# A fused linear-attention and feed-forward kernel: new ranks for its start, filling counted with two lengths, a last slice in two halves

## The chip, the cores and the metric

The kernel runs on one core of a Trainium2 chip. The metric is the device time of one execution in microseconds, here the median of 3 runs. A profiled execution stands beside it: its own time, its span (first to last instruction) and a trace of every instruction on the engines: TensorE (PE; its weight loads PEld), VectorE (DVE), ScalarE (ACT), GpSimd (POOL) and SyncE (SP), which issues most of the transfers.

## The reference

Two stages follow one another. The first is a linear attention with a decay `w` per head and channel and a bonus `u` for the current token, over 4 sequences of 768 tokens with 8 heads of 48 channels:

```python
for t in range(S):
    cur = np.einsum('bhd,bhe->bhde', u[None] * kt, vt)
    y[:, :, t] = np.einsum('bhd,bhde->bhe', rt, state + cur)
    state = w[None, :, :, None] * state + np.einsum('bhd,bhe->bhde', kt, vt)
```

The second takes its output as 3072 tokens of 384 features:

```python
h = x @ w_in                       # 384 -> 2048
g = h * np.clip(h + 3.0, 0.0, 6.0) / 6.0
return g @ w_out                   # 2048 -> 384
```

## The kernel before, in words

**Attention.** The sequence is cut into 12 chunks of 64 tokens, and each chunk into two halves (two of the four sequences each), which gives 24 steps `attention(i)`. A step scales `r` and `k` by powers of `w` (`RP`, `ks`: two products of 112x512), on the first eight steps forms their product for the bonus (`X`), scales `k` for the state (`KH`), and then has PE do two groups of small products: `first` (scores, half of the state's update, the bonus, the old state's share) and `second` (scores times `v`, the rest of the update). Between the two, DVE puts the bonus on the diagonal (L365) and copies the masked scores (L416). After `second`, DVE scales the state (`St`, L420), ACT and DVE write the step's output as a high and a low part (`x`, L429 and L430), and on the odd steps six small transfers (L439) move rows of `x` into place.

**Feed-forward.** A product in full precision is made of three products of parts: high by high, low by high, high by low. The hidden width is cut into 16 slices `f` of 128, the tokens into 6 groups `g` of 512. A unit `n` is one slice of one group. `ffn1` computes `h` with nine products (L169), ACT the rectified `t` (L457), DVE the gate (L459), ACT the high part of `g` (L461), DVE the low part (L462, recorded at the helper's L230), and `ffn2` adds nine products into three banks of PSUM (L176; bank 0 is `oa`, banks 1 and 2 are the halves of `o`). A unit of 512 tokens is in two such groups of nine products of 128x512. The first six units have 256 tokens. The weights come as 64-bit numbers; `weights(f)` loads one slice of 768 KB into `raw` and makes its high and low parts in seven operations, spread over DVE, ACT and POOL.

**What sets the order.** `Schedule` takes all of this as about 1200 operations, each with the engines that may do it and a cost on each (`add`). `order()` plays the program through with these costs, WAIT and LAND (a transfer ends LAND after its own length), and always takes on an engine the ready operation of the highest priority. The priorities of the first 561 operations are the numbers in RANKS, which reach to about the middle of the program; later ones go by the longest way to the end. The result is one fixed order for each engine. Which engine does an operation comes out of it too. SP and the engines work through their lists strictly in order.

**Filling.** Where PE has a gap of the planned order before WARM, the program puts in products that nobody reads (`warm`, L569: 128x512 in bf16 into bank `oa`), as many as fit when each lasts 0.216 us:

```python
n = int((start - free - 0.25) / 0.216)
if n > 0 and free < WARM:
```

They stand in PE's list like all else, so they are done even when the gap turns out shorter.

**The end.** The last unit is slice 15 of group 5. Its `ffn2` is done in two parts, banks 1 and 2 first and then bank 0; ACT moves bank 2 into `z` and bank 0 into `cv` (L495), DVE moves bank 1 into the other `cv` (L496), and SP sends all three (L497). After that every engine takes a branch (L601) round a fallback for unusual `w`, then SP waits for all its transfers and the engines meet at the end (L729).

Of the kernel before, what the change touches and what calls it, by code (L numbers as in the profile page):

```python
# [19 lines left out]
B, H, S, D = 4, 8, 768, 48  # L20
# [24 lines left out]
LAND = 1.8  # L45
# [134 lines left out]
def fast_path(tc, mp, pp, sb, w_hi, w_lo, b3, wm, badi, hps, o0, o12, krT, vkrt, vpt, wp, wu, wcat, out):  # L180
    nc = tc.nc
    S = Schedule()
    dma, act, dve, pool = nc.sync.dma_start, nc.scalar, nc.vector, nc.gpsimd
    eng = {"dve": dve, "pool": pool, "act": act}

    def two(name, shape, dt=F32):
        return [sb(f"{name}{q}", shape, dt, mp) for q in range(2)]
# [549 lines left out]
```

## Time and profile before

| | |
|---|---|
| median of 3 runs | 511.19 us (510.42 to 512.87) |
| the profiled execution | 511.17 us, span 509.5 us, granted TensorE clock 0.995 |
| PE busy | 494.8 us (97%), 5157 products |
| DVE busy | 300.6 us (59%) |
| ACT busy | 186.9 us (37%) |
| POOL busy | 73.2 us (14%) |
| moved by DMA | 44.38 MB |

How to read what is quoted further on. A row of the timeline is: start in us, length in us, engine, line, operation, output<-input, shapes, count, and in square brackets the idle time of the engine just before it and what ended that. A row of the chain of waits is: start, length, what the chain was doing; "issue" is time in which an engine waited for nothing that the profile shows. A row of a table by stage gives for each engine its busy us and in brackets its number of instructions that touch the stage, then the granted clock, the share of the DMA engines and GB/s. In the table of waits a row names who waited, for whom, and then us in total, how often, and the longest. In the view of one line a row has the count, then min/median/max in ns, then the first and the last start in us.

### The profile page before, as it was taken

Reading aid. Unit: us, or ns where it says so; the run is one execution under the profiler, and the core shown is the slowest. Engines: PE = TensorE matmul, PEld = TensorE weight load, DVE = VectorE, ACT = ScalarE, POOL = GpSimd, SP = SyncE. Lnnn points to the kernel's source line nnn. Section 1 sums busy time; section 2 is a strip of 40 time slices with the busy share of each in tenths; the row PEclk is TensorE's granted clock in tenths of the full one; section 3 lists DMA queues with packets and bytes.
Section 4 is the critical chain, followed back from the end, with each engine's and each line's share of the span. In section 5 each row is a group of like instructions: output and inputs, shape, how many; then the busy total and the mean of one; then the engine's idle time right before and its main releaser. Section 6 shows DMA issues by size and latency. Waiting matters only on the chain.

```text
span 509.5 us, 11797 instructions
## 1 busy us (share of the span) xinstructions
PE 494.8 (97%) x5157; PEld 393.9 (77%) x5157; DVE 300.6 (59%) x468; ACT 186.9 (37%) x295; POOL 73.2 (14%) x67
## 2 busy tenths in 40 slices
PE   9799989999999999999999999999999999999993
PEld 4566877888887888888778888778888778888882
DVE  6689999999965673534685334675333662433331
ACT  1154355556643333333233333323432333333331
POOL 1233521200001410100320001241001410000000
PEclk9999999999999999999999999999999999999997
DMA  8967573453103430200350101343100200100001
GB/s 225 263 212 218 163 225 124 161 171 124 63 0 115 132 100 1 99 0 27 119 177 8 62 1 37 103 128 100 64 0 1 99 14 15 62 1 0 1 0 68
DMA packets 14171, 44.38 MB, mean 87 GB/s; under 512 B 2561, under 2 KB 2946, under 8 KB 14114
## 3 DMA queue, kind: packets, MB, share of 16 engines
q1 hardware_dynamic: 14050, 43.50, 27.5%
q8 instruction: 42, 0.69, 0.6%
q14 instruction: 15, 0.12, 0.1%
q10 hardware_dynamic: 64, 0.07, 0.1%
HBM read 36.68 MB, written 4.72 MB: 81 GB/s over the span
## 4 chain that ended last, share of the span: by engine, by line
PE 95%; DVE 3%; issue 1%; ACT 1%; ACTq 0%
PE h L169 39%; PE o L176 25%; PE oa L176 13%; PE PP L376 10%; PE oa L569 5%; PE U L376 1%; PE o L376 1%; DVE t L459 0%; DVE z L230 0%; DVE KH L230 0%; DVE X L365 0%; DVE X L416 0%; ACT t L457 0%; PE U L325 0%; DVE z L265 0%
## 5 line engine op out<-in xcount | busy, mean ns | idle before, releaser
L169 PE MATMUL h<-x,w_hi 128*128 128x512 f32 (+1 forms) x594 | 166.8, 389 | 0.2 <-DVE t L459 0.2
L459 DVE SCALAR_TENSOR_TENSOR t<-t,h 128x512 f32<-128x512 f32 (+1 forms) x99 | 66.3, 670 | 133.7 <-ACT t L457 133.5
L176 PE MATMUL o<-g,w_hi 128*128 128x512 f32 (+1 forms) x396 | 136.2, 386 | 0.2 <-ACT g L461 0.2
L457 ACT ACTIVATE t<-h,b 128x512 f32<-128x512 f32 (+1 forms) x99 | 66.9, 676 | 187.4 <-PE h L169 187.3
L169 PEld LDWEIGHTS h<-x,w_hi 128*128 128x128 f32 x594 | 108.6, 188 | 23.4 <-DVE t L459 0.4
L230 DVE TENSOR_TENSOR g<-t,g 128x512 fp32r<-128x512 f32 (+1 forms) x99 | 69.3, 700 | 36.2 <-ACT g L461 35.7
L176 PEld LDWEIGHTS o<-g,w_hi 128*128 128x128 f32 x396 | 73.8, 188 | 16.3 <-ACT g L461 0.6
L461 ACT CAST g<-t 128x512 fp32r<-128x512 f32 (+1 forms) x99 | 60.2, 608 | 65.8 <-DVE t L459 65.7
L169 PE MATMUL h<-x,w_lo 128*128 128x512 f32 (+1 forms) x297 | 82.1, 385 | 0.0
L176 PE MATMUL oa<-g,w_hi 128*128 128x512 f32 (+1 forms) x198 | 78.3, 397 | 0.2 <-DVE g L230 0.2
L176 PE MATMUL o<-g,w_lo 128*128 128x512 f32 (+1 forms) x198 | 75.8, 383 | 0.0
L169 PEld LDWEIGHTS h<-x,w_lo 128*128 128x128 f32 x297 | 54.9, 188 | 11.6
L176 PEld LDWEIGHTS oa<-g,w_hi 128*128 128x128 f32 x198 | 37.1, 188 | 9.1 <-DVE g L230 0.7
L176 PEld LDWEIGHTS o<-g,w_lo 128*128 128x128 f32 x198 | 37.2, 188 | 7.6
L230 POOL TENSOR_TENSOR ks<-kr,IW 112x512 f32<-112x512 f32 x16 | 21.9, 1374 | 145.0 <-PE PP L376 104.9
L176 PE MATMUL oa<-g,w_lo 128*128 128x512 f32 (+1 forms) x99 | 38.0, 384 | 0.0
L376 PE MATMUL U<-vkr,KH 64*48 64x48 f32 x640 | 36.2, 204 | 0.0
L376 PEld LDWEIGHTS U<-vkr,KH 64*48 64x48 f32 x640 | 31.3, 121 | 0.0
L569 PE MATMUL oa<-ident,zw 128*128 128x512 bf16 x107 | 27.6, 403 | 0.0
L230 POOL TENSOR_TENSOR KH<-vkr,TW 128x384 f32<-128x384 f32 x15 | 15.9, 1057 | 71.5 <-PE U L376 46.9
L376 PEld LDWEIGHTS PP<-RP,ks 48*64 48x64 f32 x704 | 18.8, 132 | 7.5 <-issue 6.1
L376 PEld LDWEIGHTS PP<-X,vkr 64*48 64x48 f32 x672 | 16.5, 119 | 9.4 <-DVE X L416 3.5
(97 smaller groups left out, 413.9 us busy)
## 6 DMA issues: line engine op xcount, KB each, us to landing
raw<-wcat SPq DMA_DIRECT2D x16, 768.0 KB, 4.6
kr<-krT SPq DMA_DIRECT2D x24, 448.0 KB, 4.2
vkr<-vkrt SPq DMA_DIRECT2D x16, 576.0 KB, 4.3
outT<-cv SPq DMA_DIRECT2D x12, 256.0 KB, 2.2
vkr<-vkrt SPq DMA_DIRECT2D x6, 384.0 KB, 4.4
x<-x SPq DMA_DIRECT2D x64, 32.0 KB, 2.0
outT<-z SPq DMA_DIRECT2D x6, 256.0 KB, 3.3
part<-vpt SPq DMA_DIRECT2D x2, 336.0 KB, 6.6
```

The lines of the kernel that those rows point to most:

```text
L169: nc.tensor.matmul(h, (w_hi, w_lo)[wl][:, f, 0, 128 * j:128 * j + 128], x(j, hl), start=(m == 0 and j == 0), stop=(m == 2 and j == 2))
L176: nc.tensor.matmul(o[m], (w_hi, w_lo)[wl][:, f, 1, 128 * m:128 * m + 128], g(hl), start=(clear and k == 0), stop=(last and k == 2), skip_g ...
L230: emit = lambda e: eng[e].tensor_tensor(out=out, in0=in0, in1=in1, op=op)
L376: nc.tensor.matmul(out, lhsT, rhs, start=start, stop=True, skip_group_check=True)
L457: S.add({"act": 0.23 + 0.23 * ns}, [("h", n % 2), "b3"], [kt_], lambda e: act.activation(out=t[:, :T], in_=h[:, :T], func=AF.Relu, bias=b3 ...
L459: S.add({"dve": 0.13 + 0.28 * ns}, [("h", n % 2), kt_], [kt_], lambda e: dve.scalar_tensor_tensor(out=t[:, :T], in0=t[:, :T], scalar=6.0, ...
L461: S.add({"act": 0.18 + 0.22 * ns}, [kt_], [kg + (0,)], lambda e: act.copy(out=gt[:, 0, :T], in_=t[:, :T]))
L569: nc.tensor.matmul(o0, zw.bitcast(BF16), ident.bitcast(BF16).unsqueeze(1).broadcast_to([128, 2, 256]), start=not cleared, stop=not cleared ...
```

## The change

Four things are edited. (1) The costs: LAND is 2.0 where it was 1.8, and the lengths of the loads in `load` are raised; `order()` alone uses them. (2) RANKS is a new table of 561 numbers; with (1) it gives a new order on every engine and sends some operations to another engine. (3) Filling in gaps that begin before 5 us is counted with 0.43 us for one product, not 0.216. (4) The last unit of 512 tokens becomes two units of 256, both `ffn1` before the `ffn2` of the unit ahead of them, and bank 0 of the last group is sent from ACT's queue, not SP's.

```diff
--- before.py
+++ after.py
@@ -42,7 +42,7 @@
 
 
 WAIT = {"pe": 0.26, "act": 0.15, "dve": 0.15, "pool": 0.15, "sp": 0.15}
-LAND = 1.8
+LAND = 2.0
 LEAD = 14.0
 NR = 2
 EARLY = 8
@@ -51,26 +51,26 @@
 
 
 RANKS = """
-    217 147 558 411 543 307 554 484 517 134 442 435 425 259 450 104 111 159 518 335 473 72 372 491 428 216 274 87
...
-    382 363 38 132 48
+    502 547 127 230 523 469 556 391 46 531 500 511 438 316 458 289 459 269 116 128 144 122 86 479 236 7 373 323 535
...
+    330 447
 """
@@ -181,7 +181,7 @@
     nc = tc.nc
     S = Schedule()
     dma, act, dve, pool = nc.sync.dma_start, nc.scalar, nc.vector, nc.gpsimd
-    eng = {"dve": dve, "pool": pool, "act": act}
+    eng = {"dve": dve, "pool": pool, "act": act, "sp": nc.sync}
 
     def two(name, shape, dt=F32):
         return [sb(f"{name}{q}", shape, dt, mp) for q in range(2)]
@@ -233,14 +233,14 @@
 
     def load(i):
         q = i % 2
-        S.add({"sp": 0.43}, [], [("kT", q), ("rT", q)], lambda e: dma(kr[q], krT[i]), LEAD, dma=1.7)
+        S.add({"sp": 0.43}, [], [("kT", q), ("rT", q)], lambda e: dma(kr[q], krT[i]), LEAD, dma=1.9)
         if i < 2:
             S.add({"sp": 0.43}, [], [("kt", q)], lambda e: dma(vkr[q][:, 1:2], vkrt[i][:, 1:2]), LEAD, dma=0.75)
-            S.add({"sp": 0.43}, [], [("V", q)], lambda e: dma(Vp[i], vpt[i]), LEAD, dma=1.3)
+            S.add({"sp": 0.43}, [], [("V", q)], lambda e: dma(Vp[i], vpt[i]), LEAD, dma=2.0)
             return
         n = 2 if i < EARLY else 3
         S.add({"sp": 0.43}, [], [("V", q), ("kt", q), ("rt", q)][:n], lambda e: dma(vkr[q][:, 0:n], vkrt[i][:, 0:n]),
-              LEAD, dma=0.75 * n)
+              LEAD, dma=0.8 * n)
 
 
 
@@ -494,7 +494,9 @@
                 S.add({"act": 0.69} if m != 1 else {"dve": 0.69}, [OB[m]], [kb],
                       lambda e, m=m, o=o: act.mul(out=o, in_=ops[m], mul=1.0 / 6.0) if e == "act"
                       else dve.tensor_scalar(out=o, in0=ops[m], scalar1=1.0 / 6.0, scalar2=None, op0=ALU.mult))
-            S.add({"sp": 0.45}, [kb], [], lambda e, m=m, o=o: dma(
+
+            e = "act" if (g, m) == (NG - 1, 0) else "sp"
+            S.add({e: 0.45}, [kb], [], lambda e, m=m, o=o: eng[e].dma_start(
                 out[128 * m:128 * m + 128, 512 * g:512 * g + 512], o), dma=1.0)
 
     def flag():
@@ -531,6 +533,7 @@
 
     units = [(0, f, c, 1) for s in range(SPLIT + LAG) for f, c in ((s, 0), (s - LAG, 1)) if 0 <= f < SPLIT]
     units += [(g, f, 0, 2) for g, f0, f1 in SEGMENTS for f in range(f0, f1) if g or f >= SPLIT]
+    units[-1:] = [units[-1][:2] + (c, 1) for c in range(2)]
     pend = []
     for i in range(4):
         attend(i)
@@ -543,7 +546,7 @@
             nw += 1
         if c0 == 0 and (g, f) in beside:
             attend(beside[g, f])
-        if n == len(units) - NF:
+        if n == len(units) - NF - 1:
             flag()
         ffn1(n, g, f, c0, ns)
         pend.append((n, g, f, c0, ns))
@@ -551,6 +554,8 @@
             ffn2(*pend.pop(0))
         while ns == 2 and len(pend) > 1:
             ffn2(*pend.pop(0))
+    while len(pend) > 1:
+        ffn2(*pend.pop(0))
     for ms in ((1, 2), (0,)):
         ffn2(*pend[0], ms)
 
@@ -560,7 +565,7 @@
     pe = [d for d in done if d[2] == "pe"]
     fill = []
     for (_, free, _, _), (start, _, _, _) in zip(pe, pe[1:]):
-        n = int((start - free - 0.25) / 0.216)
+        n = int((start - free - 0.25) / (0.216 if free > 5.0 else 0.43))
         if n > 0 and free < WARM:
             fill.append((free + 0.005, n))
 
```

What the order makes of it. Filling products on PE, counted from the order, up to the place named (before / after the change):

| gap ahead of | before | after |
|---|---|---|
| the small products that make `U` from IW (L325) | 20 | 10 |
| `first` of step 0 | 6 | 7 |
| `second` of step 0 | 9 | 7 |
| `first` of step 1 | 6 | 5 |
| `second` of step 1 | 7 | 10 |
| `first` of step 2 | 15 | 17 |
| `second` of step 2 | 7 | 15 |
| all later gaps | 37 | 31 |
| all | 107 | 102 |

DVE, from the product `X` of step 0 on (row 18 in both), before. `RP_81`, `ks_84`, `X_79` are the buffers of even steps, `RP_82`, `ks_85`, `X_80` those of odd ones; `z_111`, `cv_114`, `raw_109` belong to the weights:

```order
L230 TENSOR_TENSOR X_79<-ks_84,RP_81 112x512
L230 TENSOR_TENSOR KH<-vkr_77,TW 128x384
L230 TENSOR_TENSOR RP_82<-kr_76,PQ 112x512
L230 TENSOR_TENSOR ks_85<-kr_76,IW 112x512
L365 TENSOR_TENSOR X_79<-idc,PP 128x2x4x64
L416 COPY_PREDICATED X_79<-mask,PP 128x2x4x64
L261 TENSOR_SCALAR z_111<-raw_109 128x768
L420 TENSOR_TENSOR St_88<-U,PQ 112x384
L430 TENSOR_TENSOR x_99<-PP,x_99 128x3x128
```

The same place after the change:

```order
L230 TENSOR_TENSOR X_79<-ks_84,RP_81 112x512
L230 TENSOR_TENSOR KH<-vkr_77,TW 128x384
L365 TENSOR_TENSOR X_79<-idc,PP 128x2x4x64
L416 COPY_PREDICATED X_79<-mask,PP 128x2x4x64
L230 TENSOR_TENSOR ks_85<-kr_76,IW 112x512
L230 TENSOR_TENSOR X_80<-ks_85,RP_82 112x512
L230 TENSOR_TENSOR KH<-vkr_78,TW 128x384
L420 TENSOR_TENSOR St_88<-U,PQ 112x384
L430 TENSOR_TENSOR x_99<-PP,x_99 128x3x128
L261 TENSOR_SCALAR z_111<-raw_109 128x768
```

Step 0's diagonal and mask now stand ahead of step 1's preparation; `RP_82` of step 1 has gone to POOL, its `X` and `KH` have come from POOL to DVE. By the state of step 2 (L420) DVE has 48 rows behind it, where it had 45; by the gate of unit 13 (its L459) 146, where it had 148, and POOL has two operations more.

SP's loads from the first slice of weights on, before:

```order
L250 DMA raw_109<-wcat 128x768
L236 DMA kr_75<-krT 112x1024
L236 DMA kr_76<-krT 112x1024
L355 DMA ubt<-wu 64x384 x2
L250 DMA raw_110<-wcat 128x768
L242 DMA vkr_77<-vkrt 128x768
L236 DMA kr_75<-krT 112x1024
L236 DMA kr_76<-krT 112x1024
L242 DMA vkr_78<-vkrt 128x768
L250 DMA raw_109<-wcat 128x768
```

And after:

```order
L250 DMA raw_109<-wcat 128x768
L236 DMA kr_75<-krT 112x1024
L236 DMA kr_76<-krT 112x1024
L242 DMA vkr_77<-vkrt 128x768
L355 DMA ubt<-wu 64x384 x2
L250 DMA raw_110<-wcat 128x768
L250 DMA raw_109<-wcat 128x768
L236 DMA kr_75<-krT 112x1024
L242 DMA vkr_78<-vkrt 128x768
L236 DMA kr_76<-krT 112x1024
```

The third slice of weights (the second `raw_109`) is asked for ahead of the `kr` of steps 4 and 5 and the `vkr` of step 3, where it came behind them.

ACT's end after the change; before, it ended with L495 `cv_113<-oa`, and its two operations on `g_105` were of 128x512:

```order
L457 ACTIVATE t_101<-h_66,b_63 128x256
L461 CAST g_105<-t_101 128x256
L457 ACTIVATE t_102<-h_67,b_63 128x256
L461 CAST g_103<-t_102 128x256
L495 ACTIVATE z_111<-o 128x512
L495 ACTIVATE cv_113<-oa 128x512
L499 DMA outT<-cv_113 128x512
```

Two halves stand where one unit was, and the transfer of bank 0 now is the last thing in ACT's list and gone from SP's.

36 rows, old and new, of the table RANKS are left out of this document.

## The prediction

> **What bounds the kernel now.** I read the stages first.
>
> ```profile
> 0.00:31.00 31.00, 26.73 (x501) 15.66 (x502) 19.71 (x43) 6.78 (x11) 6.40 (x15) 1.00 0.85 248
> 31.00:105.00 74.00, 71.67 (x1255) 57.26 (x1254) 71.66 (x108) 36.72 (x60) 22.98 (x16) 1.00 0.55 172
> 105.00:490.00 385.00, 385.00 (x3358) 312.51 (x3359) 205.03 (x313) 138.98 (x217) 43.86 (x37) 1.00 0.19 60
> ```
>
> From 105 to 490 us PE is busy for 385.00 of 385 us, and the change leaves that work as it is. So a microsecond won or lost before 105 us arrives at the end whole; the rest is the tail. From 31 to 105 DVE is full (71.66 of 74) and PE's 97% contains filling, so DVE paces that stage, at 71.66/108 = 0.66 us an instruction. Before 31 neither is full. The chain of waits there:
>
> ```profile
> 1.50 6.47 PE oa L569 x20
> 7.97 1.06 PE U L325 x32
> 17.02 0.28 issue
> 18.81 1.62 PE oa L569 x7
> 21.52 2.62 issue
> 24.94 3.34 PE oa L569 x15
> 28.28 0.28 PE PP L376 x8
> 30.76 1.62 PE oa L569 x7
> 32.38 0.32 PE PP L376 x10
> ```
>
> L569 is filling. The "issue" gaps have one cause. I cut windows at the ends of three of them (the third, 0.24 us, ends at 30.22); 10.97 is 256 PE instructions before the first end:
>
> ```profile
> 10.97:17.30 6.33, 6.05 (x140) 3.70 (x134) 4.50 (x8) 1.58 (x4) 2.28 (x2) 1.00 0.91 267
> 17.30:24.14 6.84, 4.19 (x127) 2.98 (x128) 5.01 (x8) 0.00 (x0) 1.18 (x1) 1.00 0.95 298
> 24.14:30.22 6.08, 5.84 (x129) 3.67 (x128) 3.92 (x6) 3.43 (x5) 1.35 (x1) 1.00 0.77 248
> q8 instruction: 1, 0.02, 5.7%
> q8 instruction: 42, 0.69, 0.6%
> ```
>
> Between gaps lie 255 and 257 PE instructions (products in flight at an edge count twice, so the first window has more): PE runs out of code after each block of 256. The fourth row is from the traffic of 21.75 to 22.9: one packet of 0.02 MB on the instruction queue; the fifth counts 42 in the run, about one for every 256 of PE's loads and products. While the DMA engines are 77 to 95% busy, a block is usable only 6.1 to 6.8 us after PE entered the block ahead of it. The Trainium skill (Runtime: NRT & Kernel Launch, Instruction fetch mechanics) has blocks of 256 too, but calls the crossing "mostly hidden"; the 2.62 us row contradicts that. By that sentence the gap would be some data's lateness, and the change could remove it.
>
> **The start, walked.** DVE's idle places, and its gate of unit 13 in the last row:
>
> ```profile
> 5.15 0.69 DVE L315 TENSOR_TENSOR IW<-PQ,rw 112x512 f32<-112x512 f32 x1
> 9.60 0.56 DVE L230 TENSOR_TENSOR KH<-vkr,TW 128x384 f32<-128x384 f32 x1 [0.68 <-ACT TW L328]
> 11.13 0.69 DVE L230 TENSOR_TENSOR RP<-kr,PQ 112x512 f32<-112x512 f32 x1 [0.97 <-DMA kr<-krT]
> 30.81 0.69 DVE L365 TENSOR_TENSOR X<-idc,PP 128x512 f32<-128x512 f32 x1 [1.92 <-PE PP L376]
> 33.62 0.55 DVE L420 TENSOR_TENSOR St<-U,PQ 112x384 f32<-112x384 f32 x1
> 104.76 0.69 DVE L459 SCALAR_TENSOR_TENSOR t<-t,h 128x512 f32<-128x512 f32 x1
> ```
>
> Fewer early fillings: IW is ready at 5.84, but PE fills until 7.97. Warm fillings last 1.62/7 = 0.23 us, so of the 6.47 us ten cost 2.3 and the ten cold ones 4.2. Ten alone end at 5.7, `U` comes 2 us earlier, `KH` no longer waits 0.68 and `first` of step 0 begins about 0.7 us earlier.
>
> DVE's new order: it did step 1's `RP` ahead of step 0's diagonal and stood 0.97 us for a load; now the diagonal goes first. `second` of step 0 gains about 1.1 us, and step 1's `first` can begin at 15.3, not 16.8.
>
> Then the code blocks take most of it back. Twelve fillings fewer (two instructions each) put the block's edge 24 instructions later. PE enters the block before it at 10.4 instead of 10.97 and, with the measured 6.33 us from 10.97 to 17.30, has the next one at 16.7; 6.84 more is 23.5, where it was 24.14. I expect the long gap to stay (2 to 2.5 us), the rest of `second` of step 1 to end at 24.0 (24.94), and 17 fillings at 0.22 us to hold PE to 27.8 (28.28). `first` of step 2 ends at 30.1 (30.76): PE is 0.7 us ahead. Next are 15 fillings where there were 7, 3.3 us, so `second` cannot begin before 33.4, where it began at 32.38: 1.0 us behind. DVE would be ready at 32.1; its St of step 2 comes at 34.6 instead of 33.62.
>
> But behind this St DVE has three instructions more. Idle waits of 1.92 and 0.97 us became work. That is 3 x 0.66 = 2.0 us, less 1.0 of delay: 1.0 ahead. Up to unit 13 DVE has two fewer in all (1.3 us), but POOL has two more, and POOL's work lengthens DVE's:
>
> ```profile
> 54.15 1.85 POOL L230 TENSOR_TENSOR w_lo<-z,w_hi 128x768 fp32r<-128x768 f32 x1 [1.81 <-DVE w_hi L270]
> 54.38 2.03 DVE L230 TENSOR_TENSOR KH<-vkr,TW 128x384 f32<-128x384 f32 x1 [0.31 <-PE U L376]
> 66.58 0.55 DVE L230 TENSOR_TENSOR KH<-vkr,TW 128x384 f32<-128x384 f32 x1
> ```
>
> The same product takes 0.55 alone and 2.03 beside POOL, so two POOL operations cost between 0 and 3 us; most of the stage's 16 meet nothing, I take 0.7. Sum at 105 us: 1.0 + 1.3 - 0.7 = 1.6 us ahead on DVE. Not all will reach PE: DVE idles only 2.3 of 74 us now, and each new wait for PE or a load costs. I take **0.9 us gained**, with bounds from 1.0 lost (PE's delay stays) to 2.3 gained (no collisions).
>
> **The tail.**
>
> ```profile
> 494.72 2.08 PE h L169 x9
> 496.88 0.70 ACT t L457
> 498.45 0.39 PE L176 MATMUL o<-g,w_hi 128*128 128x512 f32 x1
> 498.99 0.50 PE L176 MATMUL o<-g,w_hi 128*128 128x512 f32 x1 [0.15 <-ACT g L461]
> 501.20 0.39 PE L176 MATMUL oa<-g,w_hi 128*128 128x512 f32 x1
> 500.94 0.60 ACT L495 ACTIVATE z<-o 128x512 f32<-128x512 f32 x1 [2.00 <-PE o L176]
> 501.57 0.69 DVE L496 TENSOR_SCALAR cv<-o 128x512 f32<-128x512 f32 x1 [1.91 <-ACT z L495]
> 501.63 0.60 ACT L495 ACTIVATE cv<-oa 128x512 f32<-128x512 f32 x1
> 502.29 1.57 SPq L497 DMA_DIRECT2D outT<-cv  x2
> L497 SPq DMA_DIRECT2D outT<-cv x12: 338/366/987, 157.4 to 503.4; - x12
> L601 SPq COMPARE_BRANCH  x1: 50/50/50, 503.9 to 503.9; - x1
> SPq L601 <- SPq L601: 2.9, 1, 2.9
> L439 ACTq DMA_DIRECT2D x<-x x2: 605/731/857, 41.9 to 42.5; - x2
> ```
>
> Products follow each other every 2.08/9 = 0.23 us. After 498.45 nine more should begin their last at 500.52; it begins at 501.20. The last unit's chain through ACT and DVE costs 0.68 us. With halves PE has 2.08 + 1.04 us of products behind the last `ffn1`, and the chain, four operations of at most 0.70, is 2.8, for half sizes less: the 0.68 goes, and four half groups add some hundredths each. PE ends 0.64 earlier. Bank 0's last part is now half as long (0.35 us, not 0.69), so banks 1 and 2 end only 0.30 earlier; ACT's z, DVE's cv and SP's transfer of it, at 502.0, follow.
>
> SP then had a second transfer to send and took its branch at 503.9; now the branch comes behind the first. If that issue takes its 0.99 us again the branch is at 503.0, with the median 0.37 at 502.4. After the branch SP stands 2.9 us and then goes straight to the end; the new transfer must have landed by 505.3. ACT's cv ends at 501.9, its issue takes up to 0.86, and a page row gives 2.2 us to landing:
>
> ```profile
> outT<-cv SPq DMA_DIRECT2D x12, 256.0 KB, 2.2
> ```
>
> That is 505.0, just in time, so nothing new ends last. Gain 0.9 to 1.5; I take **0.9**, the row of this very place. The low bound is 0.2: ACT's own branch is now queued behind its issue, and a slow landing would end last. The Trainium skill (DMA: Bandwidth & Descriptors, Issuing engines are not separate DMA queues) says that a second issuing engine saves only the issue time; the rows agree, since the gain is SP's place in line and not a faster transfer. By it alone the transfer's move is worth SP's second issue, 1.57 - 0.99 = 0.58 us.
>
> The profiled execution took 511.17 us, 1.7 over its span and as good as the median (511.19), so both move alike: 511.2 - 0.9 - 0.9 = **509.4**.
>
> **Rivals.** (a) The head start pays in full: DVE's 2.3 us, or the 2.62 us gap vanishes with its block's edge moved, and the tail gives 1.2. For it: DVE is the full engine for 74 us. Against it: PE's gap hangs on traffic that stays. 511.2 - 2.5 - 1.2 = 507.5. (b) The overstaying fillings win: the 1.0 us behind at `second` of step 2 is kept, since step follows step through DVE and PE; 511.2 + 1.0 - 0.9 = 511.3. For it: 1.62 us of filling before 32.38 already held PE about as long as DVE needed, and now it is 3.3. Against: DVE's work ahead. (c) Slower: the third 768 KB slice now goes ahead of kr and vkr of steps 3 to 5. On SP it waits for DVE's last reading of the first slice, near 17 us, with those loads queued behind it. At the 248 to 298 GB/s of these windows that is 2.6 to 3.1 us of traffic, in front of PE's code blocks and the loads that step 3 needs; 2.9 more and the 1.0 from (b), less the tail: 511.2 + 2.9 + 1.0 - 0.9 = 514.2. It decides once a block needs above 8 us, or DVE waits for `kr`. For it: the DMA engines are 95% busy there. Against: `kr` of step 4 isn't needed before 32 us. (d) The filling doesn't do what it says: PE rests and its clock drops. The fifteen fillings after the rest of 2.62 us take 3.34, 0.22 each, so that rest did no harm; a longer one is not in the trace. The Trainium skill (TensorE: Matmul & The Clock Gate, Part 1) puts the limit near 3.4 us. If PE worked at the half clock of the first fillings (0.42 for 0.23) for 3 us of useful products, 1.5 us: 510.9.
>
> **How the numbers follow.** Forecast 0.46, (a) 0.28, (b) 0.14, (c) 0.08, (d) 0.04. The measurement can't tell less than about 0.5%, 2.6 us: below 508.6 is faster, above 513.8 slower. Faster: nearly all of (a) and a sixth of the forecast's spread (1.5 us either way), 0.34; slower: (c) and a little of (b), 0.09; the same: 0.57. The range cuts off a part of (a) below, and (c) above: 506.9 to 512.4.
>
> **What would show it.** `U` near 6.0 us and `first` of step 0 near 9.6 with no 0.68 us at `KH`; an "issue" gap of 2 us or more between 20 and 25 us, ending near 23.5 (none: (a); one that ends after 25.5: (c)); `second` of step 2 after 33; unit 13's gate on DVE near 104, where it was 104.76; PE without a gap in the last 20 us; SP's branch about 1 us nearer to PE's last product. I am wrong if PE's stage from 105 us on has gaps, if DVE's idle time before 31 us doesn't shrink, or if after the branch SP waits for ACT's transfer.

## The result, and the profile after

The changed kernel took 517.0 us (median of 4, 516.1 to 518.3) beside 510.8 us for the kernel before (4 executions): ratio 1.011, 95% interval 1.0082 to 1.0139, slower by more than 0.5%. Run again later it took 515.3 us (8 executions) beside 511.2: 1.0086, 1.0055 to 1.0117. 509.4 was forecast, with 512.4 as the upper bound; both results lie above it. The profiled execution took 516.11 us, 4.94 more than that of before.

The three stages of the changed kernel, columns as in the prediction (stretch, length, busy PE, PEld, DVE, ACT, POOL, granted clock, DMA share, GB/s):

```profile
0.00:31.00 31.00, 26.49 (x498) 15.35 (x499) 23.73 (x47) 9.25 (x14) 8.17 (x14) 0.99 0.87 260
31.00:105.00 74.00, 69.78 (x1205) 55.02 (x1204) 60.27 (x91) 34.24 (x57) 22.12 (x16) 0.96 0.50 159
105.00:490.00 385.00, 384.97 (x3395) 312.07 (x3386) 212.89 (x320) 138.36 (x216) 49.27 (x39) 1.00 0.19 62
```

Up to 31 us DVE got further than before: 47 instructions, not 43. The loss shows in the second row. DVE, full before (71.66 us, 108 instructions), is busy for 60.27 us and does 91; PE lost 1.9 us of busy time as well and shows a clock of 0.96. From 105 us on PE is full again. The chain of waits of the changed kernel says what stood in the second stage:

```profile
5.89 1.28 PE U L325 x32
8.79 0.28 PE PP L376 x8
14.51 0.28 PE o L376 x8
14.93 0.85 issue
20.42 0.73 issue
27.31 1.80 issue
29.55 5.03 PE oa L574 x15
34.58 0.31 PE PP L376 x10
42.60 1.32 issue
48.69 2.40 issue
51.09 3.11 PE h L169 x14
```

Here "issue" is a stall at the edge of one of PE's code blocks, the 256 instructions that one packet brings. There are six, 7.53 us with the 0.43 us one at 68.30, where the kernel before had 0.28 + 2.62 + 0.24 = 3.14. The first five lie behind the 444th, 700th, 955th, 1466th and 1721st of PE's loads and products: the same 256 as before, in other places of the program. These sums are of one execution each and vary: a second profile of the change (513.69 us) has five such stalls of 5.8 us and one drop of the clock, and the end of the change alone, whose start is the old one, has 1.31 us where the kernel before had 2.62. In the execution shown, the stalls of 1.80 and 2.40 us are followed by slow work: fifteen fillings take 5.03 us, where 15 x 0.22 = 3.3 were reckoned with, and fourteen products of `h` take 3.11 us where nine took 1.25 (some 1.9). Windows of the changed kernel, each cut where the trace's clock changes:

```profile
26.72:30.13 3.41, 1.61 (x53) 1.09 (x50) 3.29 (x3) 2.45 (x4) 2.46 (x1) 1.00 0.71 246
30.13:33.55 3.42, 3.42 (x10) 1.22 (x9) 2.25 (x4) 0.29 (x1) 0.00 (x0) 0.50 0.04 10
47.20:50.61 3.41, 1.49 (x48) 1.33 (x44) 2.42 (x4) 0.00 (x0) 1.19 (x1) 1.00 0.54 145
50.61:54.03 3.42, 2.94 (x14) 2.85 (x13) 1.17 (x3) 0.88 (x2) 0.00 (x0) 0.50 0.49 139
```

Twice the clock halves for exactly 3.41 us, each time behind a window of that length in which PE was busy for less than half (1.61 and 1.49 us). Half the PE time of the two slow windows, 3.42 / 2 + 2.94 / 2 = 3.2 us, is an estimate of what the halved clock cost there.

What DVE then waits for, in two windows (32 to 38 us and 50 to 56 us; the last column is the idle time ahead and who ended it):

```profile
L420 DVE TENSOR_TENSOR St<-U,PQ 112x384 f32<-112x384 f32 x1 | 0.6, 558 | 3.2 <-PE U L376 3.2
L459 DVE SCALAR_TENSOR_TENSOR t<-t,h 128x256 f32<-128x256 f32 x1 | 0.4, 423 | 2.7 <-ACT t L457 2.7
```

`St` of step 2 comes at 35.61 (33.62 before), held by the slow fillings; the gate of unit 1 at 52.86, held by the stall inside its `ffn1`. The unit that began at 131.75 now begins at 136.98, 5.23 us late. The account: 7.53 - 3.14 = 4.4 us more of stalls and 3.2 us of halved clock make 7.6, so 2.4 us of it either held up nothing or were won back by the new order; no run parts these two.

Why the code is late is told by the DMA queues. PE enters a block at 43.92 us; the packet with the next one must come before 48.69. The views of 44.0 to 45.2 (what was issued), 45.2 to 48.5 and 48.5 to 49.75 us (packets, MB, share of 16 engines):

```profile
kr<-krT SPq DMA_DIRECT2D x1, 448.0 KB
vkr<-vkrt SPq DMA_DIRECT2D x1, 384.0 KB
...
q1 hardware_dynamic: 322, 0.91, 88.9%
...
q8 instruction: 1, 0.02, 5.6%
```

Nothing moves up to 45.2 us; then 0.91 MB of loads pass, and the code packet, one of 0.02 MB, goes at 48.59, just as they have drained. It ends at 49.70 and PE runs on at 51.09. Ahead of the 1.80 us stall it is the same: PE enters the block at 21.15, the loads issued at 18.49 (`kr`), 18.86 (`vkr`) and 20.35 (`kr`) have drained by 26.5, and the packet goes at 26.52. The delay goes with what moves in it: 1.46 MB in these 5.37 us, 0.80 MB in the 2.97 us from the entry at 15.78 to that block's packet at 18.75. With nothing in flight a packet went 1.04 us after PE entered (28.88 to 29.92 in the change with light slices, a run told below).

### The profile page after: what moved, and what is told of

It reads as the page before. It is cut to its first block, busy times and chain, and to the rows that moved or that the text cites. A ratio compares the mean times of both kernels' runs of the same rounds, so it can differ in the third digit from the quotient of the medians.

```text
span 514.4 us, 11831 instructions
## 1 busy us (share of the span) xinstructions
PE 498.0 (97%) x5170; PEld 396.7 (77%) x5170; DVE 303.4 (59%) x467; ACT 188.5 (37%) x298; POOL 79.6 (15%) x69
## 4 chain that ended last, share of the span: by engine, by line
PE 95%; DVE 2%; issue 2%; ACT 0%; DVEq 0%
PE h L169 39%; PE o L176 25%; PE oa L176 13%; PE PP L376 9%; PE oa L574 5%; PE U L376 1%; PE o L376 1%; DVE X L416 0%; DVE X L365 0%; PE U L325 0%; DVE w_lo L230 0%; DVE g L230 0%; DVE z L230 0%; DVE z L261 0%; DVE cv L496 0%
## 5 line engine op out<-in xcount | busy, mean ns | idle before, releaser
L459 DVE SCALAR_TENSOR_TENSOR t<-t,h 128x512 f32<-128x512 f32 (+1 forms) x100 | 66.5, 665 | 130.5 <-ACT t L457 130.3
L169 PEld LDWEIGHTS h<-x,w_hi 128*128 128x128 f32 x600 | 109.9, 190 | 23.0
L230 DVE TENSOR_TENSOR g<-t,g 128x512 fp32r<-128x512 f32 (+1 forms) x100 | 67.8, 679 | 38.0 <-ACT g L461 37.5
L230 POOL TENSOR_TENSOR ks<-kr,IW 112x512 f32<-112x512 f32 x17 | 24.1, 1417 | 165.0 <-PE PP L376 153.8
L230 POOL TENSOR_TENSOR RP<-kr,PQ 112x512 f32<-112x512 f32 x15 | 21.6, 1438 | 14.3 <-DMA kr<-krT 11.5
```

The costliest lines, as they stand in the source:

```text
L169: nc.tensor.matmul(h, (w_hi, w_lo)[wl][:, f, 0, 128 * j:128 * j + 128], x(j, hl), start=(m == 0 and j == 0), stop=(m == 2 and j == 2))
L230: emit = lambda e: eng[e].tensor_tensor(out=out, in0=in0, in1=in1, op=op)
L459: S.add({"dve": 0.13 + 0.28 * ns}, [("h", n % 2), kt_], [kt_], lambda e: dve.scalar_tensor_tensor(out=t[:, :T], in0=t[:, :T], scalar=6.0, ...
```

## Experiments

All times are medians in us. Each ratio is against executions of the kernel before on the same chip, whose medians were 511.2 to 511.7, with its 95% interval.

| run | time | ratio |
|---|---|---|
| end of the change alone | 509.6 | 0.9962 (0.9933 to 0.9992) |
| start of the change alone | 514.3 | 1.0050 (1.0018 to 1.0081) |
| cold count alone | 510.9 | 1.0001 (0.9979 to 1.0024) |
| the change without the cold count | 517.5 | 1.0129 (1.0084 to 1.0175) |
| the change, once more | 515.3 | 1.0086 (1.0055 to 1.0117) |
| the change, slices light | 513.0 | 1.0029 (0.9999 to 1.0059) |
| before, slices light | 511.1 | 0.9983 (0.9958 to 1.0009) |
| the change, slices, kr, vkr light | 506.6 | 0.9914 (0.9883 to 0.9945) |
| before, slices, kr, vkr light | 510.5 | 0.9979 (0.9952 to 1.0006) |
| the change, kr and vkr light | 506.9 | 0.9906 (0.9872 to 0.9940) |
| the change, kr of step 7 later | 510.6 | 0.9998 (0.9969 to 1.0027) |
| the change, four fillings in one wide | 507.7 | 0.9936 (0.9909 to 0.9962) |
| before + end, four in one wide | 512.6 | 1.0037 (1.0017 to 1.0056) |
| the change, two in one wide | 525.3 | 1.0284 (1.0241 to 1.0327) |
| the change, half the fillings | 509.0 | 0.9941 (0.9914 to 0.9969) |
| four in one wide, without ScalarE's send | 507.8 | 0.9926 (0.9899 to 0.9952) |
| four in one wide, kr of step 7 later | 507.1 | 0.9918 (0.9890 to 0.9947) |

Two theories stood against each other. **Code**: PE's code packets wait behind loads, and the new order put those loads and the blocks' edges at bad places. **Order**: DVE waits for PE because of the new order itself, and the stalls only show where PE happens to stand.

**The parts.** The end alone is the kernel before with the halves and ScalarE's send:

```diff
+    units[-1:] = [units[-1][:2] + (c, 1) for c in range(2)]
...
-        if n == len(units) - NF:
+        if n == len(units) - NF - 1:
...
+            e = "act" if (g, m) == (NG - 1, 0) else "sp"
```

> The kernel before with only the end of the change: the last unit in two halves and ScalarE sending bank 0's last part. Whatever made the start slow, all theories give the same here: in the trace of the changed kernel its units run 5.72 us later than before from the 70th on and its execution ends 4.94 us later, so the end gained about 0.8 us. Expected 0.8 us less than before (0.5 to 1.2), 510.0 against 510.8. If it is no gain or a loss, the prediction's term for the tail (0.9) was wrong and the start lost less than thought.

Measured 509.6, a gain of 1.8 us, more than expected. The start alone leaves these lines out and keeps the ranks, landing times and cold count.

> The change without its end: new ranks, landing times and the cold count of fillings only. All theories: 0.8 us slower than the whole change, 517.8 (517 to 519), and 6 to 7.5 us slower than before. If it is as fast as before, the end of the change is what costs.

Measured 514.3, only 3 us slower than before, where 6 to 7.5 were expected. That was too far from the first trace to build on, so the whole change was run again beside other kernels, unchanged:

> The changed kernel once more, beside the kernel before on the same chip, since the start of the change alone came out at a ratio of 1.005 and not at the 1.0135 worked out from the first trace. Its single times should spread with the mean clock of each execution: an execution whose clock is 0.997 near 511, one at 0.985 near 517, since each drop lasts one 3.41 us piece and follows a stall. Expected median 513.5 to 516 (start alone 514.3, less 0.8 for the tail), where the first four executions gave 517.

515.3 us. The change's loss is 4 to 6 us; the first four executions were at its upper end. Single executions spread by 3.5 us (513.7 to 517.2), but not strictly by the clock as I had expected (0.995 gave 514.4, 0.993 gave 515.7).

The cold count alone, on the kernel before:

```diff
-        n = int((start - free - 0.25) / 0.216)
+        n = int((start - free - 0.25) / (0.216 if free > 5.0 else 0.43))
```

> The kernel before with only the cold count: 10 fillings ahead of U where there were 20, all else the same and in the same order. PE is free of them 2.1 us earlier and the edges of its code blocks lie 20 instructions later in the program. Theory 'code': the start gains 0.5 to 1 us up to step 1, and the stall of 2.62 us behind it takes it back, 0 to 0.8 us in all. Theory 'order' (code plays no part): the 0.68 us that KH waited, and what follows from it, arrive at the end, 0.7 to 1.5 us.

No gain: `St` of step 0 comes at 14.4 us and not 15.4, and a stall of 2.82 us at 20.06, with fifteen fillings at half clock behind it (4.93 us), takes it back, as 'code' said; `ffn1` of unit 0 begins at 33.0 where it began at 33.3. The other way round, the change without it:

> The whole change without the cold count: 20 fillings ahead of U again, so the first 2 us are as before, the edges of PE's blocks lie 20 instructions earlier in the program, and all else is in the change's order. By the walk of the prediction this costs 0.7 us against the change; by 'code' the edges fall at other places and the sum of the stalls decides, 6 to 8.5 us where it was 7.5: 514.5 to 517. Under 512 it would be the cold count that made the change slow.

517.5, in the upper part of what 'code' said: stalls of 0.87, 1.79, 1.32 and 2.86 us. The cold count isn't what made the change slow; in the change it seems to be worth some 2 us, but the two intervals overlap.

**Less traffic.** First the weight slices from the third on were cut to an eighth, in both kernels:

```diff
-... lambda e: dma(raw[f % NR], wcat[f]), dma=2.9)
+... lambda e: dma(raw[f % NR] if f < 2 else raw[f % NR][:, 0:96],
+                  wcat[f] if f < 2 else wcat[f][:, 0:96]), dma=2.9)
```

> The whole change, with the loads of weight slices 2 to 15 cut to an eighth (96 of 768 columns; the weights of those slices are then not the reference's). Same instructions in the same order, less traffic from the third slice on. Theory 'code' (PE stands at the edges of its 256-instruction blocks because the packet with the next block waits behind loads): the stalls of 0.73, 1.80 and 2.40 us at 20, 27 and 49 us shrink to under 0.5 each, with them both drops of the clock go (3.0 us), and the time falls by 5 to 8 us, to 509 to 512. Theory 'order' (the new ranks make DVE wait for PE in its own order, the stalls are only where PE happens to stand): DVE's waits stay, only 1 to 2 us fall away, 515 to 516. Theory 'clock' (the two drops are the cause, and they come from rests that the order makes): drops stay, 516.

> The kernel before, with the same loads cut. Theory 'code': the 2.62 us stall at 21.5 us lies mostly ahead of the third slice's traffic and shrinks little or by half; DVE is the full engine behind it, so the time falls by 0.5 to 2 us, to 509 to 510.3, and the changed kernel with light loads is within 2 us of it. Theory 'order': the changed kernel with light loads stays 4 to 6 us above this one.

513.0 and 511.1. The time fell by 2.3 us, but the stalls that should have gone were still in the chain of waits of the change with light slices:

```profile
25.98 2.90 issue
...
48.62 2.43 issue
```

So 'code' as I had put it, with the third slice at fault, failed. The packets said why: ahead of both stalls it was the loads of `kr` and `vkr`, at full size here, that drained as the packet went (26.19 and 48.40 us). The next pair cuts those too, from step 4 on, so these kernels leave out most of the input of those steps:

```diff
-... lambda e: dma(kr[q], krT[i]), ...
+... lambda e: dma(kr[q] if i < 4 else kr[q][:, :, 0:1], krT[i] if i < 4 else krT[i][:, :, 0:1]), ...
...
+        hh = 1 if 4 <= i < EARLY else 8
-... lambda e: dma(vkr[q][:, 0:n], vkrt[i][:, 0:n]),
+... lambda e: dma(vkr[q][:, 0:n, 0:hh], vkrt[i][:, 0:n, 0:hh]),
```

> The whole change with weight slices 2 to 15 cut to an eighth and, beside them, kr from step 4 on and vkr of steps 4 to 7 cut to one head of eight (their results are then not the reference's). With the slices alone cut, the stalls at 26 and 49 us stayed (2.90 and 2.43 us), and in each the code packet went just when the kr and vkr loads ahead of it had drained. Theory 'code, behind any load': now the packet waits for nothing after about 21 us, the stalls of 1.80, 1.32 and 2.40 us shrink to under 0.6 each, the drops of the clock behind them go, and the time is 508 to 511, within 1.5 us of the kernel before with the same cuts. Theory 'order' (DVE waits because of its own new order): DVE still idles some 10 us of the stage from 31 to 105, and the time stays 4 us or more above the kernel before with the same cuts.

> The kernel before with the same cuts. DVE is its full engine from 31 us on, so little is to be had there: 'code' and 'order' both say 508.5 to 510.5. What tells them apart is the distance of the changed kernel with the same cuts: under 1.5 us by 'code', 4 us or more by 'order'.

506.6 and 510.5: the changed kernel is 3.9 us faster than the old one under the same cuts, where 'order' said 4 us slower or worse. Stage 31 to 105 us of the change with all three light:

```profile
31.00:105.00 74.00, 73.94 (x1265) 60.60 (x1266) 69.88 (x105) 40.12 (x65) 25.97 (x19) 1.00 0.21 54
```

PE is full again and DVE nearly so (69.88 of 74 us), with the same instructions in the same order, and the clock stays at 1.00; between 16 and 60 us the longest stall is one of 0.18. 'Order' falls. The 3.9 us aren't the order's worth, though: they hold the change's end, and the old kernel keeps a stall behind loads that were left whole, with the clock at half for 3.41 us from 24.62 on. From its chain of waits:

```profile
20.60 2.89 issue
```

With `kr` and `vkr` alone cut, and the slices whole:

> The whole change with kr from step 4 on and vkr of steps 4 to 7 cut to one head of eight, and the weight slices at full size (the results of those steps are then not the reference's). It tells which loads the code packets wait behind. Cutting the slices alone brought 513.0, cutting both 506.6, where the change has 515.3. Theory 'kr and vkr alone': 507 to 508.5, the stalls of 1.32 and 2.40 us at 42 and 49 us gone. Theory 'any load': half of it, 509.5 to 512, with stalls of over 1 us left where the slices' 768 KB stand ahead of a packet.

506.9, the time of 'kr and vkr alone', though a stall of 2.37 us at 20.80 is left. The stalls at 42 and 49 us are gone. So the 'any load' theory has the stall right and the time wrong: a stall there seems to cost little by itself, and those behind 27 us, with the drops of the clock, seem to be what cost.

**One load moved.** No instruction of any other engine changes; SP sends `kr` of step 7 behind the four x transfers:

```diff
+    k7 = next(d for d in done if d[3] == late[0])
+    done.remove(k7)
+    after = [d for d in done if d[2] == "sp" and d[0] >= k7[0]][3]
+    done.insert(done.index(after) + 1, (after[0], *k7[1:]))
```

> The whole change with one load moved: SP sends kr of step 7, 448 KB, behind the four x transfers that followed it, some 3 us later. It and vkr of step 5 were the burst from 45.5 to 48.6 us behind which PE's code packet waited before the stall of 2.40 us at 48.7; the step's data isn't needed before 60 us. Theory 'code': the packet goes after vkr alone, 1.4 us earlier or more, the stall shrinks to 1.2 us or less and its drop of the clock mostly goes: 1.5 to 3 us faster than the change, 512.3 to 513.8. If the packet's lateness isn't that burst's: 515.3 as before.

510.6, 4.7 us faster than the change. The chain of waits of this kernel at that edge, where the change had 2.40 us:

```profile
46.27 0.47 issue
```

The packet went at 44.27, behind `vkr` alone, 2.78 us after PE entered the block, where it had been 4.67. The gain is more than the 1.9 us of the stall: in the profiled execution neither of the two drops of the clock is left. The second follows from the shorter stall. The first is gone because the stall ahead of it, which the moved load doesn't touch, was 1.52 us long in this execution and not 1.80. It lay whole in one window and left PE busy for more than half of that:

```profile
26.49:29.90 3.41, 1.89 (x47) 1.16 (x43) 3.41 (x3) 2.45 (x4) 2.47 (x1) 1.00 0.76 248
```

That is spread from one execution to the next, and others of this kernel (up to 515.6 us) may well have the drop.

**Fewer instructions.** Every four fillings became one on 4-byte numbers:

```diff
+        for _ in range(n // 4):
+            nc.tensor.matmul(o0[0:64], zw, ident.unsqueeze(1).broadcast_to([128, 4, 128]),
+                             start=not cleared, stop=not cleared, skip_group_check=True)
-        for _ in range(n):
+        for _ in range(n % 4):
             nc.tensor.matmul(o0, zw.bitcast(BF16), ident.bitcast(BF16).unsqueeze(1)...
```

> The whole change with every four fillings made one filling on 4-byte numbers, which should last as long as the four with a quarter of the instructions: 70 fillings before 50 us become some 25, so about 100 of PE's 1,700 instructions there fall away. The loads are untouched. Theory 'code': fewer blocks, so fewer edges: by the measured 5.4 to 6.6 us from entering one block to having the next, the stalls before 70 us sum to 2 us where they summed to 7, and the time falls to 509 to 512 from 515.3. If not the number of instructions but only the traffic counts, nothing changes: 514 to 516.

507.7, 7.5 us faster than the change with all of its work done, and faster than the kernel before. The fillings in the tile view of this run (line, engine, operation, count: least, median and most ns, first and last start, form), and behind it what is left of stalls in its chain:

```profile
L574 PE MATMUL oa<-ident,zw x38: 592/592/1112, 1.4 to 74.6; 128*64 128x512 f32 x38
L577 PE MATMUL oa<-ident,zw x26: 379/384/634, 5.1 to 75.5; 128*128 128x512 bf16 x26
```

```profile
15.67 0.78 issue
21.97 0.40 issue
46.26 0.17 issue
```

A wide filling runs as two products that follow each other every 0.43 us (19 wide ones, 38 rows; a row's 592 ns overlap the next), so four plain ones become two: 64 products and as many loads where the change had 102. The filling's time stayed (2.72 + 0.75 us for the fifteen), the clock stayed at 1.00, and the stage from 31 to 105 has 105 DVE instructions. I first read those 38 rows as 38 wide fillings of half the time each, which is what the expectation of the next run but one rests on.

The same edit on the kernel before with the new end:

> The kernel before with the end of the change and the same wide fillings. Theory 'code': its stalls were 3.1 us in all and DVE is full behind them, so little is to be had: 508.5 to 510.5, where the end alone gave 509.6. A wide filling that doesn't count as work for the clock would show as a drop behind it, 511 or more.

512.6: slower, 3 us or more above the end alone, though PE has fewer instructions and fewer edges. The chain of waits of this kernel shows one new stall, and the windows of the clock around it a drop of twice 3.41 us:

```profile
48.97 3.97 issue
```

```profile
47.30:50.71 3.41, 1.67 (x102) 1.52 (x95) 1.50 (x3) 0.00 (x0) 0.00 (x0) 1.00 0.94 336
50.71:57.54 6.83, 4.61 (x28) 4.36 (x28) 2.82 (x4) 1.29 (x2) 2.06 (x2) 0.50 0.01 2
```

PE entered the block at 44.15, and 1.61 MB of loads, `kr`, `vkr` and a slice issued in that time, passed before the packet went at 50.40, 6.2 us later. The expectation's 511 or more had the number, but for another reason: wide fillings do keep the clock up, it stayed at 1.00 in the run before this one. So it isn't the number of instructions that decides but where an edge falls against a burst of loads; with plain fillings the old start had been luckier.

To part the filling's time from its instructions, two more runs of the change:

```diff
-        for _ in range(n):
+        for _ in range(n // 2):
+            nc.tensor.matmul(o0[0:64], zw, ident.unsqueeze(1).broadcast_to([128, 4, 128]), ...
+        for _ in range(n % 2):
             nc.tensor.matmul(o0, zw.bitcast(BF16), ...
```

> The whole change with every two fillings made one on 4-byte numbers. In the run with four made one, a wide filling lasted 0.43 us warm and 0.85 cold, as long as two plain ones and not four; so there the filling's time was halved along with its instructions, and two causes are mixed. Here the time of the filling stays and only its instructions are halved, some 70 fewer of PE's before 50 us. Theory 'code': the edges of the blocks move and the sum of the stalls with them, 509 to 513 where the change has 515.3. Theory 'overstay' (the fillings hold PE too long, and shortening them is what helped): no gain, 514 to 516.5.

```diff
-        for _ in range(n):
+        for _ in range(n // 2 + n % 2):
             nc.tensor.matmul(o0, zw.bitcast(BF16), ...
```

> The whole change with every two plain fillings made one plain one: the same number of PE instructions at the same places as with two made one wide, so the same edges, but half the filling's time. Theory 'code': within 1.5 us of the run with two made one wide. Theory 'overstay': 2 us or more below it, at 508 to 511, since the fifteen fillings ahead of second of step 2 then last 1.8 and not 3.3 us and the seventeen ahead of first 2.0 and not 3.8.

525.3 and 509.0. With a wide filling being two products, the first run has the change's instructions and twice its filling time; the expectation had it the other way round, so its numbers don't apply. The four runs make a table all the same:

| fillings | their instructions | their time | us |
|---|---|---|---|
| as in the change | all | all | 515.3 |
| four in one wide | about half | all | 507.7 |
| every second left out | about half | half | 509.0 |
| two in one wide | all | twice | 525.3 |

Halving the instructions is worth 7.5 us; halving the time as well adds nothing (509.0). The last two don't compare cleanly, since the profile with half the fillings has a drop of the clock (3.41 us from 30.46, behind a window with 0.64 us of PE work). But `St` of step 2 says the same: with the filling's whole time in wide ones it comes earlier than in the kernel before (33.62), and with half the time at 32.71. Its row in the run with four in one wide:

```profile
32.34 0.56 DVE L420 TENSOR_TENSOR St<-U,PQ 112x384 f32<-112x384 f32 x1 [0.31 <-PE U L376]
```

So at the change's length the fillings overstaying isn't what costs. At twice the length it is. The chain of that kernel, at the two long fillings that took 3.78 and 5.03 us in the change:

```profile
27.57 7.01 PE oa L574 x16
36.83 6.15 PE oa L574 x14
```

Here PE is held by filling, and the chain has no "issue" row above 0.1 us before 84 us.

**One loss or two.** Both remedies at once:

> The change with both remedies: four fillings made one wide (507.7 us alone) and kr of step 7 sent later (510.6 alone, where the change has 515.3). Theory 'code': both take away the same loss, PE's stalls at the edges of its blocks and the drops of the clock behind them; with the wide fillings 0.78, 0.40 and 0.17 us of them are left, none near that load's burst, so the second remedy has nothing to add: 507 to 508.5. If the two causes were separate, their gains of 7.5 and 4.7 us would add to 503.

507.1, and not 503: the moved load and the fewer instructions take away the same loss. This version and the one with wide fillings alone are the fastest that do all of the work; the 0.6 us between them is within their intervals.

**The tail.** Wide fillings with SP sending the last bank:

```diff
-            e = "act" if (g, m) == (NG - 1, 0) else "sp"
+            e = "sp"
```

> The whole change with four fillings made one wide (507.7 us), but the last output bank is sent by SP again and not by ScalarE. In the traces with ScalarE's send its issue took 0.4 us once and 1.5 us in three others, and then SP stood after its branch until that transfer had landed, 4.2 to 5.0 us and not 2.9. So the send is worth about nothing: expected within 0.7 us of 507.7, and SP's wait after its branch 2.9 to 3.2 us. If ScalarE's send is the gain that the prediction took it for, 0.5 to 1 us slower.

507.8 against 507.7, and SP stands 3.07 us after its branch. ScalarE's send is worth nothing here. Rows of ScalarE's issue, of SP's branch and of what SP does next, of the changed kernel and then of the kernel with the end alone:

```profile
L499 ACTq DMA_DIRECT2D outT<-cv x1: 1507/1507/1507, 507.5 to 507.5; - x1
L606 SPq COMPARE_BRANCH  x1: 50/50/50, 508.1 to 508.1; - x1
L606 SPq EVENT_SEMAPHORE  x8: 17/17/17, 512.3 to 512.9; - x8
```

```profile
L498 ACTq DMA_DIRECT2D outT<-cv x1: 385/385/385, 500.1 to 500.1; - x1
L605 SPq COMPARE_BRANCH  x1: 50/50/50, 500.8 to 500.8; - x1
L605 SPq EVENT_SEMAPHORE  x8: 17/17/17, 504.3 to 504.8; - x8
```

In the changed kernel the issue takes 1.51 us, its transfer has landed at 511.85, and SP goes on at 512.3, 4.2 us after its branch; with the old ranks the issue takes 0.39 and SP waits 3.5. Over the profiles of all runs, counted from the start of `ffn1` of unit 97: without the send the execution ends after 18.2 to 19.1 us (6 profiles); with it and the new ranks after 18.2 to 19.0 (11 profiles, the issue 1.5 to 1.8 us in each); with it and the old ranks after 17.43 (both profiles, 0.39 us). The medians fit that: the start alone, without the new end, isn't slower than the whole change (1.0050 and 1.0086). Why ScalarE's issue takes four times as long under the new ranks wasn't tried and stays open.

## Why the prediction was wrong

- **The start up to step 1: right, the gain even larger.** `U` at 5.89 (forecast near 6.0), no wait at `KH`, `first` of step 0 at 8.79 (9.6; 10.44 before), `first` of step 1 at 14.51 (15.3).
- **"Then the code blocks take most of it back ... I expect the long gap to stay (2 to 2.5 us)": this is the step that failed.** I took the time from entering a block to having the next as a constant of 6.1 to 6.8 us, and counted one gap, ahead of 24 us. It isn't a constant: it is 1.0 us until the packet goes if nothing is in flight and up to 6.4 us behind loads (19.82 to 26.19 in the change with light slices), and at the six stalls 2.3 to 2.6 us from there to PE's next instruction. The change moved the edges and the bursts, so every edge up to 60 us had to be laid against the loads issued at that time. In place of one gap of 2 to 2.5 us there were five up to 51 us, 7.1 us together, and a sixth behind them.
- **"Sum at 105 us: 1.0 + 1.3 - 0.7 = 1.6 us ahead on DVE": failed with it.** DVE's work would have paced the stage only with PE's code there. DVE idled 13.7 of 74 us. With all loads light DVE does 105 instructions there (91 in the change, 108 before); what the order by itself is worth stays open, since the 3.9 us between the two kernels under these cuts hold the end and the old kernel's stall as well.
- **"so `second` cannot begin before 33.4": right in kind.** It began at 34.58; `St` at 35.61, not 34.6. The 1.2 us between are the clock.
- **Rival (a), 0.28: its sign came and its time didn't.** No gap of 2 us or more was left between 20 and 25 us (0.73, ending at 21.15), but the edges had moved and the long stalls with them, to 27.31 and 48.69.
- **Rival (c), 0.08: the right kind of mechanism with the wrong load.** Loads in front of the code blocks it was, 5 us and more; but with the slices cut to an eighth the two long stalls stayed and 2.3 us came back, with `kr` and `vkr` cut 8.4. Its sign, a gap that ends after 25.5 us, was there (29.11), and its point of decision, a block that needs above 8 us, nearly: 7.96 us from 21.15 to 29.11.
- **Rival (d), 0.04: was part of it.** I argued that a rest of 2.62 us had done no harm and only a longer one could. Rests of 1.80 and 2.40 us, 1.92 of the second in one window, did: what counts is the share of a fixed window and not the length of a rest. Its price, 1.5 us for one drop, was about right (1.7 and 1.5 by the estimate above); there were two.
- **Rival (b), 0.14: not borne out.** `second` of step 2 did come late, but by the clock. With the same filling time and few stalls `St` of step 2 comes at 32.34, 1.3 us earlier than in the kernel before, and half the filling's time gained nothing beyond the instructions.
- **The tail, "I take 0.9": 0 under the new ranks, 1.3 under the old.** Counted from `ffn1` of unit 97, PE ends 0.57 us earlier (0.64 forecast) and SP's branch comes 0.8 to 1.6 us earlier (1 forecast). But "its issue takes up to 0.86" was 1.51, so the transfer lands at 511.85 and SP waits for it, which the prediction named as a sign of being wrong. In the pair of profiles this left 0.8 us; over all profiles nothing.

## What to carry to other kernels

A kernel of many small TensorE instructions has a second stream of loads, its own code, and an order made without it can lose more than it wins: lay the edge of every 256-instruction block against the load bursts issued in the microseconds after PE enters the block ahead of it. What helps is cheap: send a load that isn't due a few microseconds later, or do filler work in fewer, longer instructions. Neither is sure (the same wide fillings made the old order some 3 us slower): both are judged by the "issue" rows of the chain of waits, and an equally busy-looking version may only have been lucky in its edges. When one change moves work, read the stalls and the clock of the new trace before blaming the order.

## What the runs showed of the hardware

- **A code packet goes behind the kernel's loads.** It went 1.04 us after PE entered a block with nothing in flight, 2.97 us after when 0.80 MB of loads moved in between, 5.37 us after with 1.46 MB, and 6.37 us after with 1.50 MB (the last in the change with light slices). At 43.92 us the queues were empty, and two loads issued 0.5 and 0.9 us later, 832 KB together, still went first (4.67 us). Why is open. The Trainium skill (Runtime: NRT & Kernel Launch, Instruction fetch mechanics) has the fetch hidden behind the sequencer's issue time; these rows contradict it for blocks of small products.
- **The clock is decided by windows of 3.41 us at fixed places.** The two windows ahead of the drops were busy for 1.61 and 1.49 of 3.41 us (47 and 44%), a third, in the old kernel with wide fillings, for 1.67 (49%). But the limit isn't sharp: in the change with `kr` and `vkr` light a window with 1.65 us (48%) had no drop behind it. In the kernel before the rest of 2.62 us fell across an edge and both windows stayed above half, without a drop:

```profile
19.27:22.68 3.41, 2.22 (x48) 1.26 (x47) 3.34 (x6) 0.00 (x0) 0.40 (x1) 1.00 0.99 364
22.68:26.09 3.41, 1.95 (x28) 1.27 (x28) 1.57 (x4) 1.29 (x2) 1.01 (x1) 1.00 0.83 241
```

  (Its clock halves at 503.96 us, 141 x 3.413 us behind 22.68.) The Trainium skill (TensorE: Matmul & The Clock Gate, Part 1) calls the window free-running and 3413 ns long, which agrees; that a window need only be idle for about half is from these rows.
- **The time of single executions goes with the clock.** Of 117 executions of the kernel before, the 33 with a mean clock of 0.995 or more took 510.1 us on average, the 16 with 0.990 or less 513.6. That the place of the windows makes the difference would fit, but wasn't tried; and the mean clock counts half clock behind PE's last product too, as at 503.96 us above.
- **A product of 4-byte numbers over 512 columns ran as two rows 0.43 us apart**, with two weight loads, where one of 2-byte numbers takes 0.22.
